# A Sinkhorn-sorted attention followed by a mixer: a fixed VectorE order, later channel results, one spin tile and split row sums

## The chip, the core and the metric

The kernel runs on one core of a Trainium2 chip. A core has TensorE (PE: matmuls, with weight loads listed apart as PEld), VectorE (DVE), ScalarE (ACT), GpSimd (POOL) and SyncE (SP), which run side by side, each with its own queue, and 16 DMA engines. The metric is device time in microseconds, as a median over runs. Before the change it is 265.28 us, the median of 6 runs (264.29 to 265.69).

## The reference

Four batches, eight heads, 768 positions, head width 64, model width 512. Cut to what matters:

```python
P = sort_net                                  # 4 x 8 x 8 x 8
for _ in range(5):
    P = np.exp(P - P.max(-1)); P = P / P.sum(-1); P = P / P.sum(-2)
k_sorted = einsum('bhij,bhjcd->bhicd', P, k_b)    # blocks of 96 positions, mixed by P
v_sorted = einsum('bhij,bhjcd->bhicd', P, v_b)
attn = softmax(q_b @ k_sorted.T / 8)              # within a block
x = attn @ v_sorted                               # then heads side by side: 4 x 768 x 512
a1 = alpha1 * x + beta1
u = x + lam * einsum('ts,bsd->btd', w_tok, a1)
a2 = alpha2 * u + beta2
out = u + lam * (relu(a2 @ w_ch1) @ w_ch2)        # hidden width 2048
```

## The kernel before

All of it is unrolled Python; there are no loops on the chip. The order of the work on an engine is either the order in which it is written (an `Engine` wrapper, L55 to L71, keeps it while its `fixed` is true) or, with `fixed` false and for DMAs on SP, chosen by a planner that simulates the program with its own costs. TensorE and POOL are in written order throughout. ScalarE is until L811. VectorE is until L817, `dve.fixed = False`; all that VectorE does after that, the planner orders. The planner also hands out the buffers.

PSUM has two pools: psA, two slots of two banks (`psa`), and psB, four slots of one bank (`psb`). Each tile takes a slot and keeps it until its last reader is done; the next tile that gets this slot waits for that.

**The head** (to about 42 us): five Sinkhorn rounds on a 32 x 8 x 8 tile (L244 to L265), with `spin` matmuls on TensorE whose result nobody reads, each group in a fresh psA tile. `mixing_heads` (L312) builds bigH, the mixing matrices of batch 0, in three pieces of 2, 2 and 4 heads, one at each `next`. For each of four pairs of heads (loop at L769), `mix_k0`/`mix_v0` mix keys and values on TensorE, and the results are copied out by ScalarE (first part) and VectorE (second); `sc0` computes scores and their exponential, `turn_v0` transposes values, and `pv0` multiplies by values and normalizes on VectorE (a reciprocal and a product) into `x_of[0]`. Then `prep_wtok` transposes w_tok by 128-column blocks, which `sort_wtok` has regrouped on POOL; `mixes(1, n)` mixes the values of batch 1 in three parts; `prep_rs` sums the rows of w_tok by 36 matmuls with a column of ones.

**The token half** of a batch (`moe_a`, or L790 to L816 for batch 0): six row tiles, each with `tok_part` (6 matmuls into psB), `moe_scale` and `moe_rest` (two VectorE operations; the second adds into the fp32 tile `u`, and ScalarE casts it to fp16). POOL has prepared `u` by `moe_rows` and `moe_start`. After three rows `moe_turn` transposes the fp16 tile, on TensorE for batch 0 and by DMA on SP for the others, and applies alpha2 and beta2: four VectorE operations that make a2T.

**The channel half**: `moe_h(b, hf)` computes 16 hidden tiles (4 matmuls each, relu on ScalarE); `moe_ch` has 16 matmuls per row tile, whose result VectorE multiplies by lam and adds to u, and SP stores.

**The weave** (L539): the channel half of batch b - 1 is a generator of units, and `weave` puts so many units (0.65 for a hidden tile, 0.216 for a channel matmul, in microseconds by the writer's count) between the steps of batch b's attention: key mixes, `scores(h4)`, `values(h4)`. `values` is, for each of two halves: matmuls, a reciprocal, products into x or xs; and for the last two groups three copies from xs to the last partitions of x (two on VectorE, one on ScalarE). Then `moe_a(b)` follows, and the rest of `moe_ch(b - 1, 1)`.

All operations are recorded by the wrapper, so that the profile gives one line, L65, for nearly all; tiles tell them apart: m_ps, k_ps, v_ps (mixes), sc_ps (scores), x_ps (values), tok_ps, h_ps, ch_ps, rs_ps, wtok_ps.

Of the kernel before, what the change touches and what calls it, by code (L numbers as in the profile page):

```python
# [1 line left out]

# [14 lines left out]
def kernel(  # L17
# [67 lines left out]
    def psa(shape, dtype, name):  # L85
        return psA.tile(shape, dtype, name=name, tag="psA")

    def psb(shape, dtype, name):
        return psB.tile(shape, dtype, name=name, tag="psB")
# [124 lines left out]
                    ident16[0:BH, 0:BH].rearrange("p (b h) -> p b h", h=H).unsqueeze(3).to_broadcast([BH, B, H, NB]),  # L214
                )

    def spin(ps, n):
        src = ident16[:].unsqueeze(1).to_broadcast([128, 4, 128])
        for _ in range(n):
            pe.matmul(ps, ident16[:], src, start=True, stop=True)  # L220


    def turn_q(b, h4, copy):
# [20 lines left out]
    for it in range(5):  # L244
        act.activation(P32[:], P32[:], AF.Exp)
        dve.tensor_reduce(rsum[:], P32[:], AXX, ALU.add)
        dve.reciprocal(rsum[:], rsum[:])
        dve.tensor_tensor(
            P32[:], P32[:], rsum[:].unsqueeze(2).to_broadcast([BH, NB, NB]), ALU.mult
        )  # L250
        dve.tensor_reduce(csum[:], P32[:].rearrange("p i j -> p j i"), AXX, ALU.add)
        dve.reciprocal(csum[:], csum[:])
        dve.tensor_tensor(
            (P16 if it == 4 else P32)[:], P32[:],
            csum[:].unsqueeze(1).to_broadcast([BH, NB, NB]), ALU.mult,
        )
        if it < 4:
            with nc.allow_low_precision(reason="sums of zeros and a one"):
                mask(it)
        if it == 2:  # L260
            prep_ab2()
        if it > 2:
            for h4 in ((0,), (1, 2, 3))[it - 3]:
                turn_q(0, h4, act.copy)
        spin(psa([128, 512], FT, "spin_ps")[:], (8, 0, 7, 4, 2)[it])  # L265

    def load_w1(gs):
        for g in gs:
# [43 lines left out]
    def mixing_heads():  # L312
        pjs = psb([NB, H, NB], FT, "pj_ps")
        for i in range(NB):
            pe.matmul(pjs[:, :, i], P16[:, i, :], ident16[0:BH, 0:H], start=True, stop=True)
        spin(psa([128, 512], FT, "spin_ps")[:], 1)
        pj = const([NB, H, NB], F16, "pj")
        dve.tensor_copy(pj[:], pjs[:])
        rep = psb([128, H, NB], FT, "rep_ps")
        pe.matmul(  # L320
            rep[:].rearrange("p h i -> p (h i)"), eb16[:].rearrange("p j r -> p (j r)"),
            pj[:].rearrange("p h i -> p (h i)"), start=True, stop=True,
        )
        spin(psa([128, 512], FT, "spin_ps")[:], 2)
        for hs in (slice(0, 2), slice(2, 4), slice(4, 8)):
            yield
            dve.tensor_tensor(
                bigH[:, hs, :, :],
                rep[:, hs, :].unsqueeze(3).to_broadcast([128, hs.stop - hs.start, NB, 16]),
                mskt[:].unsqueeze(1).unsqueeze(1).to_broadcast([128, hs.stop - hs.start, NB, 16]),  # L330
                ALU.mult,
            )
        yield
# [177 lines left out]
    def attention_steps(b, first, less=0.0):  # L511
# [24 lines left out]
        yield 2.4 - less, lambda: values(2)  # L536
        yield 2.4 - less, lambda: values(3)

    def weave(fill, steps):  # L539

        for gap, step in steps:
            filled = 0
            while filled < gap:
                took = next(fill, None)
                if took is None:
                    break
                filled += took
            step()

    w_tokT = const([128, NT, S], F16, "w_tokT")  # L550
# [21 lines left out]
            act.copy(dst[:, :, 0:96], pst[:, 0:TAIL].rearrange("p (kt x) -> p kt x", x=96))  # L572
            dve.tensor_copy(dst[:, :, 96:128], pst[:, TAIL:S].rearrange("p (kt x) -> p kt x", x=32))

    def prep_rs():
        rps = psb([128, NT], FT, "rs_ps")
        for kt in range(NT):
            for ks in range(NT):
                pe.matmul(
                    rps[:, kt:kt + 1], w_tokT[:, ks, kt * 128:(kt + 1) * 128], ones16[:],  # L580
                    start=(ks == 0), stop=(ks == NT - 1),
                )
        act.copy(rs[:], rps[:])

    u_of = {}
    u16_of = {}
# [58 lines left out]
    def moe_turn(b, hf, ps=psb):  # L645
        u16, a2T = u16_of[b], a2T_of[b]
        if b > 0:
            uT = uT_of[b][hf]
            for m in range(3):
                turned.append(nc.sync.dma_start_transpose(uT[:, :, m * 128:(m + 1) * 128], u16[:, 3 * hf + m, :]))  # L650
            for ci in range(CT):
                dve.tensor_scalar(
                    a2T[hf][:, ci, :], uT[:, ci, :], ab2col[:, ci:ci + 1], ab2col[:, CT + ci:CT + ci + 1],
                    op0=ALU.mult, op1=ALU.add,
                )
            return
        for cp in range(CT // 2):
            ups = ps([128, 2, 384], F16, "uT_ps")
            for cc in range(2):
                ci = 2 * cp + cc  # L660
                for m in range(3):
                    pe.transpose(
                        ups[:, cc, m * 128:(m + 1) * 128],
                        u16[:, 3 * hf + m, ci * 128:(ci + 1) * 128], ident16[:],
                    )
            for cc in range(2):
                ci = 2 * cp + cc
                if cp == 0:
                    act.activation(
                        a2T[hf][:, ci, :], ups[:, cc, :], AF.Identity,  # L670
                        bias=ab2col[:, CT + ci:CT + ci + 1], scale=ab2col[:, ci:ci + 1],
                    )
                else:
                    dve.tensor_scalar(
                        a2T[hf][:, ci, :], ups[:, cc, :], ab2col[:, ci:ci + 1], ab2col[:, CT + ci:CT + ci + 1],
                        op0=ALU.mult, op1=ALU.add,
                    )

    def moe_a(b):
        ahead = b + 1 if b < B - 1 else None  # L680
        moe_start(b)
        for kt in range(NT):
            if ahead and kt < 3:
                mixes(ahead, kt)
            tok_part(b, kt)
            moe_scale(b, kt)
            if kt % 3:
                moe_rest(b, kt - 1)
            if kt % 3 == 2:
                moe_rest(b, kt)  # L690
                moe_turn(b, kt // 3)
        if ahead:
            with tc.issue_after(turned[-1].ins):
                regroup_v(ahead)
# [3 lines left out]
    def moe_h(b, hf, which=range(HT)):  # L698
# [3 lines left out]
        for m in which:  # L702
# [4 lines left out]
                    start=(ci == 0), stop=(ci == CT - 1),  # L707
                )
            act.activation(hT_of[(b, hf)][m], hps[:], AF.Relu)
            yield 0.65  # L710

    def moe_ch(b, hf, kks=range(3)):
        hT = hT_of[(b, hf)]
        for kk in kks:
            kt = 3 * hf + kk
            last = b == B - 1 and kt == NT - 1
            u32 = u_of[(b, kt)]
            for lo, hi in ((0, 384), (384, C)) if last else ((0, C),):
                cps = psb([128, hi - lo], FT, "ch_ps")
                for m in range(HT):  # L720
# [2 lines left out]
                        start=(m == 0), stop=(m == HT - 1),  # L723
                    )
                    if m < HT - 1:
                        yield 0.216
                dve.tensor_tensor(cps[:], cps[:], lamB[:, lo:hi], ALU.mult)
                dve.tensor_tensor(u32[:, lo:hi], cps[:], u32[:, lo:hi], ALU.add)
                nc.sync.dma_start(out[b, kt * 96:(kt + 1) * 96, lo:hi], u32[0:96, lo:hi])
                (nc.scalar if last else nc.sync).dma_start(  # L730
                    out[b, TAIL + kt * 32:TAIL + (kt + 1) * 32, lo:hi], u32[96:128, lo:hi]
                )
                yield 0.216

    def run(units):
        for _ in units:
            pass


    ets = {}  # L740
# [10 lines left out]

    x_of[0] = moep.tile([128, NT, C], F16, name="x128", tag="x128", bufs=2)
    big = mixing_heads()
    for _ in range(3):
        next(big)
    k_copy, v_copy = mix_k0(0), mix_v0(0)
    k_copy(0, act.copy)
    k_copy(1, dve.tensor_copy)
    v_copy(0, act.copy)
    v_copy(1, dve.tensor_copy)  # L760
    next(big)
    load_raw(1, 1)
    load_w1(range(2))
    for n in range(3):
# [4 lines left out]
    for h4 in range(H4):  # L769
        sc0(h4)  # L770
        turn_v0(h4, dve.tensor_copy if h4 < 3 else act.copy)
        if h4 == 3:
            mixing_matrices(1, psb)
        if h4 > 0:
            pv0(h4 - 1, 0)
            pv0(h4 - 1, 1)
        if h4 < 3:
            k_copy, v_copy = mix_k0(h4 + 1), mix_v0(h4 + 1)
            k_copy(0, act.copy)
            k_copy(1, dve.tensor_copy)  # L780
            v_copy(0, act.copy)
            v_copy(1, dve.tensor_copy)
    prep_wtok(range(0, 2))
    pv0(3, 0)
    prep_wtok(range(2, 4))
    pv0(3, 1)
    prep_wtok(range(4, 6))
    mixes(1, 0)
    prep_rs()
    moe_rows(0, range(NT))  # L790
    moe_start(0)
    load_q(1)
# [21 lines left out]
        moe_scale(0, kt)  # L814
    for kt in (4, 5):
        moe_rest(0, kt)  # L816
    dve.fixed = False  # L817

    stack = ExitStack()
    for eng in order:  # L820
# [1 line left out]
    pe.fixed = True  # L822
    run(moe_h(0, 0, range(7)))
    moe_turn(0, 1)
    for n in range(3):
        mix_k(1, gs=(n,))
        run(moe_h(0, 0, range(7 + 3 * n, 9 + 3 * n)))
        turn_q(1, n, dve.tensor_copy)
        run(moe_h(0, 0, range(9 + 3 * n, 10 + 3 * n)))
    turn_q(1, 3, dve.tensor_copy)  # L830
    stack.close()
    pool.tensor_copy(gate[32:64, :], Vs[1][32:64, 0, 0:2])
# [11 lines left out]
    for b in range(1, B):  # L844
# [11 lines left out]
        moe_rows(b, range(5, NT))  # L856
        moe_a(b)
        run(moe_ch(b - 1, 1, (1, 2)))
        if b < B - 1:
            moe_rows(b + 1, range(3))  # L860
        if b == 1:
# [40 lines left out]
```

## Time and profile before

| | us |
|---|---|
| median of 6 runs | 265.28 |
| profiled execution, its own time | 264.45 |
| its span | 262.7 |
| TensorE busy | 249.9 |
| VectorE busy | 146.6 |
| ScalarE busy | 132.4 |
| POOL busy | 93.3 |
| TensorE busy of the first 42 us | 36.4 |

The span is the time from the first to the last instruction of one execution. A busy TensorE isn't TensorE at its peak, since matmuls overlap. A line of the timeline gives start, duration, engine, the operation with what it writes and reads, and in brackets the idle time of the engine before it and what ended that. A line of waits gives who waited for whom, and then the total, the number of times and the longest. The chain is the work that ended last, followed backwards. A wait for several things is put down to the one that came last, which is not always the one that was needed.

### The profile page before, as it was taken

What the parts mean: (1) busy time and instruction counts of PE and PEld (TensorE: products, weight loads), DVE (VectorE), ACT (ScalarE), POOL (GpSimd) and SP (SyncE); (2) the same over time, 40 slices, a digit from 0 to 9 for tenths busy, and PEclk for the clock granted to TensorE, in tenths of its full rate; (3) what the DMA queues carried; (4) which work ended last, traced back from release to release, by engine and by line L of the source; (5) the groups of instructions that cost most, each with busy time, mean ns of one, the idle gap of its engine ahead of it and who ended that gap; (6) DMA issues with size and microseconds to landing.
All of it is one profiled execution on the core that took longest, in us unless ns stands there. A gap on an engine that the chain in (4) does not pass through costs nothing.

```text
span 262.7 us, 5105 instructions
## 1 busy us (share of the span) xinstructions
PE 249.9 (95%) x2032; PEld 140.3 (53%) x2047; DVE 146.6 (56%) x323; ACT 132.4 (50%) x240; POOL 93.3 (36%) x101
## 2 busy tenths in 40 slices
PE   5988899999999799999999999999999999999993
PEld 1577645665555344554566445654665445545542
DVE  5776787682066796852625797644537973042033
ACT  3577887758622451484176632862574326505600
POOL 8433996000886395006830880203002700000000
PEclk9999999999999999999999999999999999999999
DMA  5999999999699734795999156991200342012012
GB/s 77 187 208 256 196 191 240 207 216 136 114 179 151 198 61 64 191 113 85 204 201 129 45 82 131 157 72 40 84 0 2 82 93 65 2 40 80 2 40 80
DMA packets 62327, 30.88 MB, mean 118 GB/s; under 512 B 48792, under 2 KB 58016, under 8 KB 62304
## 3 DMA queue, kind: packets, MB, share of 16 engines
q0 software_dynamic: 22912, 15.60, 40.4%
q1 hardware_dynamic: 39296, 14.90, 34.0%
q8 instruction: 16, 0.26, 0.4%
q10 hardware_dynamic: 96, 0.07, 0.1%
q14 instruction: 7, 0.06, 0.1%
HBM read 32.78 MB, written 8.65 MB: 158 GB/s over the span
## 4 chain that ended last, share of the span: by engine, by line
PE 74%; DMA 12%; DVE 8%; issue 2%; POOL 2%; ACT 1%; DVEq 0%; POOLq 0%
PE h_ps L65 31%; PE ch_ps L65 28%; DMA raw<-in_v_dram 10%; PE tok_ps L65 7%; DVE u L65 3%; PE sc_ps L65 2%; PE x_ps L65 2%; DVE tok_ps L65 2%; PE k_ps L65 1%; DMA a2T<-u 1%; DVE a2T L65 1%; PE v_ps L65 1%; PE q_ps L65 1%; DVE ch_ps L65 1%; POOL qn L65 1%
## 5 line engine op out<-in xcount | busy, mean ns | idle before, releaser
L65 PE MATMUL h_ps<-a2T,W1p 128*128 128x384 bf16 x512 | 89.0, 326 | 0.7 <-DVE u L65 0.6
L65 ACT ACTIVATE hT<-h_ps 128x384 bf16<-128x384 f32 x128 | 60.3, 492 | 55.6 <-PE h_ps L65 55.1
L65 PE MATMUL ch_ps<-W2p,hT 128*128 128x512 bf16 (+2 forms) x385 | 85.6, 370 | 1.0 <-issue 0.3
L65 PEld LDWEIGHTS <-W1p 128*128 128x128 bf16 x512 | 48.5, 98 | 32.5 <-issue 1.2
L65 PEld LDWEIGHTS <-hT 128*128 128x128 bf16 x400 | 37.6, 98 | 41.0
L65 DVE TENSOR_TENSOR ch_ps<-ch_ps,lamB 128x512 f32<-128x512 f32 (+2 forms) x25 | 16.9, 676 | 51.0 <-PE ch_ps L65 40.7
L65 POOL TENSOR_SCALAR u<-b1lB,rs 128x512 f32<-128x512 f32 x18 | 28.0, 1561 | 29.8 <-DMA out_dram<-u 23.4
L65 POOL TENSOR_TENSOR u<-x,u 128x512 f32<-128x512 f16 x22 | 25.3, 1182 | 29.2 <-DVE x L65 29.0
L65 PE MATMUL tok_ps<-x,w_tokT 128*128 128x512 f16 x144 | 32.9, 379 | 1.1 <-DVE x L65 1.1
L65 ACT ACTIVATE et<-sc_ps 96x768 f16<-96x768 f32 x32 | 24.0, 802 | 13.7 <-PE sc_ps L65 13.7
L65 ACT CAST u<-u 128x512 f16<-128x512 f32 x24 | 14.7, 618 | 20.9 <-DVE u L65 20.9
L65 PEld LDWEIGHTS <-w_tokT 128*128 128x128 f16 x180 | 15.0, 97 | 18.1 <-issue 1.4
L65 DVE CAST kT<-k_ps 64x512 f16<-64x512 f32 x30 | 20.6, 686 | 5.1 <-PE k_ps L65 4.7
L65 DVE RECIPROCAL recip<-x_ps 96x8 f32<-96x8 f32 (+1 forms) x32 | 6.2, 194 | 30.1 <-PE x_ps L65 30.1
L65 DVE TENSOR_TENSOR x<-x_ps,recip 96x512 f16<-96x512 f32 (+2 forms) x32 | 17.7, 554 | 1.0
L65 DVE TENSOR_TENSOR tok_ps<-tok_ps,a1lB 128x512 f32<-128x512 f32 x24 | 16.6, 693 | 2.6 <-PE tok_ps L65 2.6
L65 DVE TENSOR_TENSOR u<-tok_ps,u 128x512 f32<-128x512 f32 x24 | 16.4, 689 | 2.3 <-POOL u L65 0.7
L65 DVE TENSOR_TENSOR u<-ch_ps,u 128x512 f32<-128x512 f32 (+2 forms) x25 | 16.7, 670 | 0.8
L65 POOL DMA_DIRECT2D qn<-in_q_dram x16 | 14.0, 913 | 2.5 <-DMA raw<-in_v_dram 1.7
L65 POOL COPY gate<-Vs 32x2 f16<-32x2 f16 x2 | 0.4, 176 | 40.6 <-DMA Vs<-vscr 40.6
L65 PEld LDWEIGHTS <-et 96*128 96x128 f16 (+1 forms) x288 | 12.0, 105 | 3.0 <-DVE x L65 0.3
L65 PE MATMUL x_ps<-Vs,et 96*128 96x65 f16 (+1 forms) x288 | 12.7, 197 | 0.3 <-DVE xs L65 0.2
(88 smaller groups left out, 181.9 us busy)
## 6 DMA issues: line engine op xcount, KB each, us to landing
out_dram<-u SPq DMA_DIRECT2D x23, 192.0 KB, 2.4
raw<-in_k_dram POOLq DMA_DIRECT2D x8, 384.0 KB, 9.6
raw<-in_v_dram POOLq DMA_DIRECT2D x8, 384.0 KB, 8.0
vscr<-vA SPq DMA_DIRECT2D x6, 384.0 KB, 5.1
Vs<-vscr SPq DMA_DIRECT2D x6, 384.0 KB, 8.9
W1p<-in_moe_w_ch_dram POOLq DMA_DIRECT2D x4, 512.0 KB, 13.7
W2p<-in_moe_w_ch_dram POOLq DMA_DIRECT2D x4, 512.0 KB, 16.8
qn<-in_q_dram POOLq DMA_DIRECT2D x4, 384.0 KB, 8.6
```

What stands on the lines that cost most here:

```text
L65: ins = getattr(self.eng, name)(*args, **kwargs)
```

## The change

`dve.fixed = False` is gone, so that VectorE runs in written order to the end. What is taken of a channel tile is now a job of its own, `finish`; in the weave a job is written only once 1.2 (in the units' count) has gone by after the tile's last matmul. `moe_affine` is split from `moe_turn` for batches 1 to 3: half 0 is written behind all six rows, half 1 behind the last two channel tiles of the batch before. All spin matmuls write one tile, `rep` moves from psB to psA, and the k copies of the first pair of heads stand ahead of bigH's last two pieces. In the head's loop the next pair's key mix stands between the two halves of `pv0`, and the first block of w_tok is transposed there in the last turn. The row sums run over blocks in the outer loop, four blocks before `mixes(1, 0)` and two after it; only the first of the 36 matmuls has the start flag. Between 42 and 60 us one hidden tile comes ahead of the first key mix of batch 1, and none is left between the last two `turn_q`.

```diff
-    def spin(ps, n):
+    idle = psa([128, 512], FT, "spin_ps")
+    def spin(n):
...
-            pe.matmul(ps, ident16[:], src, start=True, stop=True)
+            pe.matmul(idle[:], ident16[:], src, start=True, stop=True)
...
-        rep = psb([128, H, NB], FT, "rep_ps")
+        rep = psa([128, H, NB], FT, "rep_ps")
...
+    late = []
+
+    def settle(took=None):
+        for job in late:
+            job[0] = 0 if took is None else job[0] - took
+        while late and late[0][0] <= 0:
+            late.pop(0)[1]()
+
+    def advance(unit, lag):
+        took, job = unit
+        settle(took)
+        if job:
+            late.append([lag, job])
+        return took
+
     def weave(fill, steps):
...
-                took = next(fill, None)
-                if took is None:
+                unit = next(fill, None)
+                if unit is None:
                     break
-                filled += took
+                filled += advance(unit, 1.2)
             step()
...
-    def prep_rs():
-        rps = psb([128, NT], FT, "rs_ps")
-        for kt in range(NT):
-            for ks in range(NT):
+    def prep_rs(rps, part):
+        for ks in part:
+            for kt in range(NT):
                 pe.matmul(
                     rps[:, kt:kt + 1], w_tokT[:, ks, kt * 128:(kt + 1) * 128], ones16[:],
-                    start=(ks == 0), stop=(ks == NT - 1),
+                    start=(ks + kt == 0), stop=(ks + kt == 2 * NT - 2),
                 )
-        act.copy(rs[:], rps[:])
+        if part[-1] == NT - 1:
+            act.copy(rs[:], rps[:])
...
 in moe_turn, for b > 0:
-            for ci in range(CT):
-                dve.tensor_scalar(
-                    a2T[hf][:, ci, :], uT[:, ci, :], ab2col[:, ci:ci + 1], ab2col[:, CT + ci:CT + ci + 1],
-                    op0=ALU.mult, op1=ALU.add,
-                )
             return
...
+    def moe_affine(b, hf):
+        uT, a2T = uT_of[b][hf], a2T_of[b][hf]
+        for ci in range(CT):
+            dve.tensor_scalar(
+                a2T[:, ci, :], uT[:, ci, :], ab2col[:, ci:ci + 1], ab2col[:, CT + ci:CT + ci + 1],
+                op0=ALU.mult, op1=ALU.add,
+            )
...
 in moe_a, behind the six rows:
+        moe_affine(b, 0)
...
+    def finish(b, kt, cps, lo, hi):
+        u32 = u_of[(b, kt)]
+        last = b == B - 1 and kt == NT - 1
+        dve.tensor_tensor(cps[:], cps[:], lamB[:, lo:hi], ALU.mult)
+        dve.tensor_tensor(u32[:, lo:hi], cps[:], u32[:, lo:hi], ALU.add)
+        nc.sync.dma_start(out[b, kt * 96:(kt + 1) * 96, lo:hi], u32[0:96, lo:hi])
+        (nc.scalar if last else nc.sync).dma_start(
+            out[b, TAIL + kt * 32:TAIL + (kt + 1) * 32, lo:hi], u32[96:128, lo:hi]
+        )
...
 in moe_ch, whose six lines from the product to the stores are gone:
-                        yield 0.216
+                        yield 0.216, None
+                yield 0.216, partial(finish, b, kt, cps, lo, hi)
...
     def run(units):
-        for _ in units:
-            pass
+        for unit in units:
+            advance(unit, 0.0)
+        settle()
...
     big = mixing_heads()
-    for _ in range(3):
-        next(big)
+    next(big)
+    next(big)
     k_copy, v_copy = mix_k0(0), mix_v0(0)
     k_copy(0, act.copy)
     k_copy(1, dve.tensor_copy)
+    next(big)
+    next(big)
     v_copy(0, act.copy)
     v_copy(1, dve.tensor_copy)
-    next(big)
...
     for h4 in range(H4):
         sc0(h4)
         turn_v0(h4, dve.tensor_copy if h4 < 3 else act.copy)
-        if h4 == 3:
-            mixing_matrices(1, psb)
         if h4 > 0:
             pv0(h4 - 1, 0)
+        if h4 < 3:
+            k_copy = mix_k0(h4 + 1)
+            k_copy(0, act.copy)
+            k_copy(1, dve.tensor_copy)
+        else:
+            mixing_matrices(1, psb)
+            prep_wtok(range(0, 1))
+        if h4 > 0:
             pv0(h4 - 1, 1)
         if h4 < 3:
-            k_copy, v_copy = mix_k0(h4 + 1), mix_v0(h4 + 1)
-            k_copy(0, act.copy)
-            k_copy(1, dve.tensor_copy)
+            v_copy = mix_v0(h4 + 1)
             v_copy(0, act.copy)
             v_copy(1, dve.tensor_copy)
-    prep_wtok(range(0, 2))
+    prep_wtok(range(1, 2))
     pv0(3, 0)
     prep_wtok(range(2, 4))
     pv0(3, 1)
     prep_wtok(range(4, 6))
+    rps = psb([128, NT], FT, "rs_ps")
+    prep_rs(rps, range(4))
     mixes(1, 0)
-    prep_rs()
+    prep_rs(rps, range(4, NT))
...
-    dve.fixed = False
...
     run(moe_h(0, 0, range(7)))
     moe_turn(0, 1)
+    run(moe_h(0, 0, range(7, 8)))
     for n in range(3):
         mix_k(1, gs=(n,))
-        run(moe_h(0, 0, range(7 + 3 * n, 9 + 3 * n)))
+        run(moe_h(0, 0, range(8 + 3 * n, 10 + 3 * n)))
         turn_q(1, n, dve.tensor_copy)
-        run(moe_h(0, 0, range(9 + 3 * n, 10 + 3 * n)))
+        run(moe_h(0, 0, range(10 + 3 * n, min(11 + 3 * n, HT))))
     turn_q(1, 3, dve.tensor_copy)
...
         moe_a(b)
         run(moe_ch(b - 1, 1, (1, 2)))
+        moe_affine(b, 1)
```

## The prediction

> **What bounds the kernel now.** I first read the page: busy time by engine, then the slices.
>
> ```profile
> PE 249.9 (95%) x2032; PEld 140.3 (53%) x2047; DVE 146.6 (56%) x323; ACT 132.4 (50%) x240; POOL 93.3 (36%) x101
> PEclk9999999999999999999999999999999999999999
> ```
>
> TensorE is busy for 249.9 of 262.7 us, and its granted clock stays at the top, so nothing is to be had from the clock. No edit takes matmuls away, so what can be won is idle TensorE time: 12.8 us. The busy time by stretch says where it lies:
>
> ```profile
> 20.00:31.00 11.00, 9.48 (x193) 7.96 (x190) 8.19 (x26) 8.71 (x15) 7.08 (x8) 1.00 1.11 235
> ...
> 60.00:85.00 25.00, 24.63 (x221) 13.79 (x223) 8.76 (x22) 12.06 (x23) 15.35 (x16) 1.00 1.33 141
> 85.00:108.50 23.50, 21.52 (x120) 10.43 (x121) 18.56 (x38) 9.73 (x15) 12.97 (x10) 1.00 0.55 121
> 108.50:146.00 37.50, 37.32 (x318) 21.60 (x321) 19.08 (x40) 20.73 (x40) 12.85 (x15) 1.00 1.19 145
> ```
>
> The first pair of numbers is the stretch and its length, the next TensorE's busy time. From 108.5 us to 258 it is idle for 0.55 us (0.18, 0.05, 0.16, 0.05 and 0.11 by stretch), and 4.0 us at the end are the last results on their way out. Only one stretch after the head has a hole, 85 to 108.5 us: 1.98 us. The head, up to 42 us, holds the other 5.7. Then the waits of TensorE, by what ended them:
>
> ```profile
> PE tok_ps L65 <- DVE x L65: 1.1, 1, 1.1
> PE h_ps L65 <- DVE u L65: 0.6, 1, 0.6
> PE v_ps L65 <- DMA raw<-in_v_dram: 0.6, 1, 0.6
> ```
>
> Three single waits, each in its own place: the first token matmul of batch 1 (at 89.18 us), one hidden tile of batch 2's weave (at 108.52) and batch 1's first value mix (at 31.38). The chain shows the last:
>
> ```profile
> 13.99 17.35 DMA raw<-in_v_dram
> 31.33 0.04 issue
> 31.38 0.61 PE v_ps L65 x2
> 31.98 0.91 PE rs_ps L65 x36
> 32.89 1.32 PE tok_ps L65 x6
> ```
>
> The load of batch 1's values lands at 31.33, whatever TensorE does before; the head is bound by that load, not by the engines.
>
> **Part 1: row sums split.** Before, TensorE ends its last w_tok transpose at 30.79 (29.90 plus 0.89 in the timeline), waits 0.59 for the load, mixes, and only then does 36 row-sum matmuls, 0.91 us by the chain or 25 ns each. After, 24 of them come ahead of the mix: 24 x 25 = 0.61 us, from 30.79 to 31.40. So the wait is filled, and tok_part(0, 0) starts at 31.38 + 0.44 + 12 x 25 ns = 32.1 instead of 32.75: **0.6 us**. This needs the first four blocks of w_tokT; their last copy ends at 30.79 on VectorE. Is the 0.6 kept? The u rows hang on the ScalarE copy of rs, queued behind the copy of the mix, and that copy doesn't move (32.02 to 33.03); so VectorE's first scaling stays at 34.55. But its second waits for TensorE (0.73 us before 35.97), and can start at 35.4; from there rows, casts and the turn at 40.09 all move by 0.57. POOL's rows (35.25, 36.5, ...) are early enough.
>
> Here the Trainium skill speaks against the move. "TensorE: Matmul & The Clock Gate", section "LDWEIGHTS (loading the stationary operand)", gives columns / 1.2 ns for a weight load, 107 ns for 128 columns, and every row-sum matmul has a load of its own. By that, 24 take 2.56 us, the mix would slip by 2.0 us to 33.4, the rs copy with it, and the gain would turn into a loss of about 1.4. The rows of weight loads read 97 ns each in fact, but they overlap: 36 went through in 0.91 us. I take the measured 25 ns.
>
> **Part 2: the head's reordering** (rep in the psA pool, k copies ahead of bigH's later heads, pv0's halves interleaved, first w_tok block earlier). In the loop, score to score takes 3.63 us (17.17, 20.80, 24.44), for 3.0 us of TensorE work; the score waits for the VectorE copy of kT, which is queued behind two attention results (0.70 each: 0.22 plus 0.47 start to start). With one of them moved behind that copy, I estimate 0.5 us less in each of two turns. Against it: the first score's second half now needs the slot that rep holds until bigH's last part. That part is 0.68 us and moves ahead of the v copy (k copy at 13.91, then 0.34, 0.35 and 0.68 to 15.3), so the first score ends at 15.6 instead of 15.2, and the transposes behind it at 16.2 instead of 15.9: 0.3 lost. Bounds on TensorE's arrival at the mix: 0.3 later to 1.1 earlier (w_tok's last regrouping on POOL ends at 28.70, and 12 transposes after it take 0.89). **Zero** in the sum, since an early arrival only waits for the load; a late one would eat as much of part 1's 0.6. The single spin tile costs nothing: its matmuls are a warm-up on one engine, and one slot is as good as two in turn.
>
> **Part 3: one hidden tile ahead of batch 1's key mix** (42 to 60 us). The same 64 matmul groups of 0.65 us, otherwise ordered. It moves the first q transposes by 0.65 - 0.57, from 49.66 to 49.74; the weight load there ended a wait on the qn load, so without this the earlier clock of part 1 would be lost there. At the end two q turns stand back to back: two 0.59 us pieces of TensorE beside two 0.56 us copies. Zero.
>
> **Part 4: VectorE in written order, channel results six matmuls later** (6 x 0.216 = 1.296, over the lag of 1.2). I counted where each result now stands among the attention steps. In batches 2 and 3 every one stands where the profile already has it: the first two before the values of group 0, the third before group 1, the fourth after group 3. In batch 1 two move. Before, VectorE takes the third channel product at 82.83 ahead of the reciprocal, and the fourth at 88.19 ahead of the copies that the token matmul waits for:
>
> ```profile
> 82.83 0.70 DVE L65 TENSOR_TENSOR ch_ps<-ch_ps,lamB 128x512 f32<-128x512 f32 x1 [2.21 <-PE ch_ps L65]
> ...
> 87.86 0.41 DVE L65 TENSOR_TENSOR xs<-x_ps,recip 96x256 f16<-96x256 f32 x1
> 88.19 0.68 DVE L65 TENSOR_TENSOR ch_ps<-ch_ps,lamB 128x512 f32<-128x512 f32 x1
> 88.90 0.47 DVE L65 COPY x<-xs 32x256 f16<-32x256 f16 x2
> ```
>
> After, the fourth stands behind the copies (0.70 less), but the third stands between group 2 and group 3, still ahead of them. The row starts at 83.02 (x_ps at 82.56 plus the 0.46 of the other groups). By start-to-start distances: group 2 0.23 + 0.61 + 0.22 + 0.35 + 0.37, copies 0.75, third result 0.73 + 0.61, group 3 0.23 + 0.61 + 0.22 + 0.35 + 0.44, first copy 0.28: 6.00, so the token matmul starts at 89.02 instead of 89.18. **0.16 us**, not the 1.15 that the wait is worth: VectorE is the bound in these six microseconds. TensorE's 0.15 us wait at 85.81 falls within it.
>
> **Part 5: moe_affine moved.** Before, the second affine stands ahead of the second channel result:
>
> ```profile
> 105.89 1.25 DVE L65 TENSOR_SCALAR a2T<-a2T,ab2col 128x384 bf16<-128x384 f16 x4 [3.00 <-DMA a2T<-u]
> 107.05 0.70 DVE L65 TENSOR_TENSOR ch_ps<-ch_ps,lamB 128x512 f32<-128x512 f32 x1
> 107.78 0.69 DVE L65 TENSOR_TENSOR u<-ch_ps,u 128x512 f32<-128x512 f32 x1
> ```
>
> VectorE waits 3.00 us for a transposing DMA while the channel matmuls ended at 104.7; the slot is freed at 108.47, and TensorE starts its next hidden tile at 108.52. After, the result is taken at 104.75 to 106.15, and the tile need not wait: **0.6 us**. In batches 2 and 3 nothing waited here: 0. What stands behind the affine's wait now: the affine itself and the key copies (at 108.39 before). With the first affine behind the sixth row, the last cast starts at 99.8 instead of 101.48, so the transposes land nearer 104.1 than 105.8. The first affine ends at 101.1 instead of 100.85, against a first use at 104.7 - 0.7.
>
> **Sum:** 0.6 + 0.16 + 0.6 = 1.36 us, 262.7 to 261.3 of span. The profiled execution took 264.45, 1.75 around its span; the same step from there is 263.1. The six runs' median of 265.28 lies 0.83 above that execution, so I put the step on the median: **263.9 us**.
>
> **Rivals.** (a) *The full wait goes.* If the third result, too, falls outside the row before the token matmul, 1.15 goes instead of 0.16: 262.9. For it: it is the largest of the three waits. Against: the count above puts that result six matmuls after its last, four ahead of group 3. (b) *Part 1 is lost again*, at the qn load (49.66, no slack beyond 0.1) or through a late head: 0.76 stays, 264.5. (c) *It doesn't do what it says*: the POOL row at 89.30, which waits for an output store that the transposes on SP hold back until 86.52, stays where it is; its u row is first used at 92.03. If the slots behind it bind, all gains up to there end there. Against: the fifth token tile, at 94.5, needs its slot at 92.7, so 1.8 us are to spare. That gives 265.3. (d) *Slower: the SP queue and the strict order meet.* SP's order is still a plan. If it sets the store of the second channel result ahead of the second three transposes, they can issue only from 105.5, take 3 x 1.86 (11.18 for six) and 1.2 to land: 112.3. The affine (1.25) and three key copies (2.08) behind it then end at 115.6, and the third key mix, at 113.59 - 1.36 = 112.2, needs their slot: 3.4 lost, 2.0 net, 267.3. It decides once the landing passes 108.9, 3.1 us later than now. Against: casts are ready before that result.
>
> **How the numbers follow.** A measurement tells this kernel from no change at about 0.3%, 0.8 us: faster is below 264.48, slower above 266.08. Chances: the forecast 0.54, its own range 263.3 to 264.5; (a) 0.10; (b) 0.14, half of it under the bound; (c) 0.11; (d) 0.11. So faster 0.54 + 0.10 + 0.07 = 0.71, same 0.07 + 0.11 = 0.18, slower 0.11. Leaving out (d) and the lower half of (a), the range is 262.8 to 265.5: above (c) by 0.2 for the spread of the runs.
>
> **What would show it.** Right: tok_ps starting near 32.1; no wait of v_ps longer than before with 24 row sums ahead of it; tok_ps of batch 1 still waiting for VectorE, about 1 us, near 88.4; no h_ps wait on u near 107; batches 2 and 3 the same length. Wrong: a v_ps mix later than 31.5; a q_ps wait on qn; key copies waiting behind a2T for a transpose; longer stretches after 110 us.

## The result

The changed kernel takes 263.41 us, the median of its runs (262.24 to 267.66), against 264.65 for the kernel before beside it: a ratio of 0.9953, with a 95% interval of 0.9939 to 0.9967. Forecast were 263.9 against 265.28, a ratio of 0.9948. The profiled execution took 263.21, with a span of 261.4; the sum on record gave 263.1 and 261.3. The total is right; below it shows that several of its terms were not, and that they offset each other by luck. In five of the changed kernel's executions, the ones above 266 us, TensorE's mean granted clock was 0.985 to 0.990; a median "at full clock" below is one of executions with a mean of 0.995 or more.

The page after, busy time and granted clock:

```profile
PE 248.8 (95%) x2032; PEld 140.4 (54%) x2047; DVE 146.0 (56%) x323; ACT 133.1 (51%) x240; POOL 93.2 (36%) x101
PEclk9999999999999999999999999999999999999999
```

The work is the same, 2032 matmuls. Busy time by stretch, with the same columns as before (the stretch, its length, then TensorE first):

```profile
20.00:31.00 11.00, 9.47 (x203) 8.43 (x204) 8.38 (x27) 8.41 (x13) 6.11 (x8) 1.00 1.12 236
...
60.00:85.00 25.00, 24.63 (x223) 13.99 (x226) 9.25 (x26) 12.55 (x23) 15.35 (x16) 1.00 1.34 144
85.00:108.50 23.50, 22.25 (x127) 10.89 (x128) 19.92 (x38) 9.78 (x16) 12.92 (x10) 1.00 0.63 140
108.50:146.00 37.50, 37.34 (x318) 21.45 (x320) 18.86 (x41) 21.31 (x41) 14.09 (x16) 1.00 1.16 136
```

Between 85 and 108.5 us TensorE is idle for 1.25 us instead of 1.98. The weave of batch 2 behind it is as full as it was. The waits of TensorE, by what ended them:

```profile
PE v_ps L66 <- DMA raw<-in_v_dram: 0.7, 1, 0.7
PE v_ps L66 <- DVE x L66: 0.6, 1, 0.6
PE tok_ps L66 <- DVE x L66: 0.5, 1, 0.5
```

The wait of h_ps for VectorE is gone. The load wait is still there, longer by 0.1, and the wait of 1.15 before the first token matmul now stands in two pieces, 0.60 and 0.54. Where TensorE stands at the same point of the work, read from its timelines:

| point | before | after | gap | won or lost since the row above |
|---|---|---|---|---|
| first token matmul, batch 0 | 32.75 | 32.92 | +0.17 | 0.17 lost |
| first hidden tile | 42.05 | 42.23 | +0.18 | 0 |
| first score of batch 1 | 60.33 | 60.01 | -0.32 | 0.50 won |
| first token matmul, batch 1 | 89.18 | 88.64 | -0.54 | 0.22 won |
| second half's hidden tiles | 104.71 | 104.30 | -0.41 | 0.13 lost |
| third key mix of batch 2 | 113.59 | 112.35 | -1.24 | 0.83 won |
| span | 262.7 | 261.4 | -1.3 | 0.06 won |

The sum on record had 0.6 won in the first row, nothing in the third, 0.16 in the fourth and 0.6 in the sixth.

### The profile page after: what moved, and what is told of

Its sections match the earlier page's. It is cut to its first block, busy times and chain, and to the rows that moved or that the text cites. A ratio compares the mean times of both kernels' runs of the same rounds, so it can differ in the third digit from the quotient of the medians.

```text
span 261.4 us, 5106 instructions
## 1 busy us (share of the span) xinstructions
PE 248.8 (95%) x2032; PEld 140.4 (54%) x2047; DVE 146.0 (56%) x323; ACT 133.1 (51%) x240; POOL 93.2 (36%) x101
## 4 chain that ended last, share of the span: by engine, by line
PE 76%; DMA 11%; POOL 7%; DVE 3%; issue 2%; POOLq 0%; DVEq 0%
PE ch_ps L66 30%; PE h_ps L66 30%; PE tok_ps L66 9%; DMA wt<-in_moe_w_tok_dram 7%; DMA qn<-in_q_dram 4%; PE sc_ps L66 2%; PE x_ps L66 2%; POOL wtp L66 2%; POOL raw L66 2%; POOL u L66 2%; PE k_ps L66 1%; DVE x L66 1%; PE q_ps L66 1%; PE v_ps L66 1%; POOL qn L66 1%
## 5 line engine op out<-in xcount | busy, mean ns | idle before, releaser
L66 ACT ACTIVATE et<-sc_ps 96x768 f16<-96x768 f32 x32 | 24.0, 802 | 12.8 <-PE sc_ps L66 12.8
L66 DVE TENSOR_TENSOR u<-tok_ps,u 128x512 f32<-128x512 f32 x24 | 15.8, 684 | 1.4 <-POOL u L66 1.1
L66 ACT CAST vA<-v_ps 128x1024 f16<-128x1024 f32 x9 | 9.0, 1008 | 8.3 <-PE v_ps L66 8.3
```

The lines of the kernel that those rows point to most:

```text
L66: ins = getattr(self.eng, name)(*args, **kwargs)
```

## The experiments

The theory is the sum on record: the split, the third result and the affine bring the gain, and parts 2 and 3 nothing. The rivals: the split is worth nothing where TensorE is late anyway, part 2 costs something, and part 3 brings something.

**No split** (no_split). All 36 row sums behind the mix:

```diff
+    mixes(1, 0)
     rps = psb([128, NT], FT, "rs_ps")
-    prep_rs(rps, range(4))
-    mixes(1, 0)
-    prep_rs(rps, range(4, NT))
+    prep_rs(rps, range(NT))
```

> The changed kernel with all 36 row sums behind the value mix again. Theory (part 1: 24 row sums of 25 ns fill a wait for the value load): token part of batch 0 starts 24 x 25 ns = 0.6 us later after the mix, the time is 0.6 us more than the changed kernel's, so about 0.6 less than before (ratio 0.9975 to before). Rival (the load's own scatter or the head's order hides it): same time as the changed kernel, ratio about 0.995.

263.72 us, ratio 0.998 (0.9943 to 1.0016); at full clock 263.20 (eight of twelve), no worse than the changed kernel's 263.35. The profile says why nothing was lost. TensorE's timeline in the changed kernel first, then in this one:

```profile
30.08 0.83 PE L66 MATMUL wtok_ps<-ident,wtp 128*128 128x128 f16 x12
30.75 0.74 PE L66 MATMUL rs_ps<-ones,w_tokT 128*128 128x1 f16 x24
32.18 0.61 PE L66 MATMUL v_ps<-raw,bigV 128*128 128x512 f16 x2 [0.69 <-DMA raw<-in_v_dram]
32.62 0.44 PE L66 MATMUL rs_ps<-ones,w_tokT 128*128 128x1 f16 x12
32.92 1.46 PE L66 MATMUL tok_ps<-x,w_tokT 128*128 128x512 f16 x6
```

```profile
29.27 0.49 PE L66 MATMUL wtok_ps<-ident,wtp 128*128 128x128 f16 x6 [0.96 <-DVE w_tokT L66]
...
31.58 0.59 PE L66 MATMUL v_ps<-raw,bigV 128*128 128x512 f16 x2
32.01 1.26 PE L66 MATMUL rs_ps<-ones,w_tokT 128*128 128x1 f16 x36
33.14 1.02 PE L66 MATMUL tok_ps<-x,w_tokT 128*128 128x512 f16 x4
```

In the changed kernel the row sums do run inside the wait, of which 0.69 us is left, and token work starts 0.74 after the mix instead of the 1.37 before the change. But here there is no wait to fill: TensorE itself is late, because it waited 0.96 us for VectorE at 29.27. VectorE's timeline in the same kernel, and POOL's:

```profile
27.27 1.27 DVE L66 TENSOR_TENSOR bigP<-mskb,red 128x128 f16<-128x128 f16 x1
28.46 0.58 DVE L66 TENSOR_TENSOR bigV<-mskv,red 128x128 f16<-128x128 f16 x1
28.97 0.24 DVE L66 COPY w_tokT<-wtok_ps 128x192 f16<-128x192 f16 x1
```

```profile
24.18 4.72 POOL L66 COPY wtp<-wt 128x1152 f16<-128x1152 f16 x6 [4.04 <-DMA wt<-in_moe_w_tok_dram]
...
27.25 1.14 POOL L66 COPY wtp<-wt 128x1152 f16<-128x1152 f16 x1
```

bigP, a product of two SBUF tiles, takes 1.27 us. Its two later instances in the changed kernel take 0.29. Of POOL's six copies in the first row one runs beside it, from 27.25 to 28.39 (second row), and bigP ends 0.14 later. In the changed kernel's own profile the copies begin 0.7 us later, and bigP and bigV take 0.41 and 0.59. bigP took 1.16 to 1.27 in no_split, affine_between and third_result_later, and 0.49 in old_hidden_order (the last three stand further down). The new theory: VectorE and POOL exclude each other here, and what that costs depends on when w_tok lands.

**A shorter POOL copy** (short_pool_copies), which should let VectorE in sooner if it waits only for the running instruction: each of the six copies is written as three (the larger ones of 128 x 1152 as 128 x 384, the smaller ones of 128 x 384 as 128 x 128).

```diff
-            pool.tensor_copy(
-                t_[:, :, :, lo:hi],
...
+            for ts in (slice(0, 2), slice(2, 4), slice(4, 6)):
+                pool.tensor_copy(
+                    t_[:, ts, :, lo:hi],
```

> The changed kernel with each of POOL's six w_tok copies cut in three. Theory (a VectorE product with both inputs in SBUF waits until the running POOL copy ends): no bigP over 0.75 us, the w_tok transpose's wait falls by about half a microsecond, if the cut copies don't take longer in all; ratio 0.992 to 0.995. Rival (bigP waits for something else): bigP still takes about 1.2 us in some executions, ratio 0.995 or more.

The opposite. Six of its eleven executions took 263.1 to 264.0 us (a ratio of 0.995, 0.9931 to 0.9968, no gain on the changed kernel's 0.9953), and five took 269.0 to 269.8 with a clock of 0.973 to 0.979. The profile is of one of these five; of the six there is none. VectorE's and POOL's timelines:

```profile
27.29 4.56 DVE L66 TENSOR_TENSOR bigP<-mskb,red 128x128 f16<-128x128 f16 x1
31.77 0.28 DVE L66 TENSOR_TENSOR bigV<-mskv,red 128x128 f16<-128x128 f16 x1
```

```profile
27.13 2.12 POOL L66 COPY wtp<-wt 128x384 f16<-128x384 f16 x6
29.21 1.27 POOL L66 TENSOR_TENSOR a1lB<-a1lB,lamB 128x512 f32<-128x512 f32 x1
30.44 1.26 POOL L66 TENSOR_TENSOR b1lB<-b1lB,lamB 128x512 f32<-128x512 f32 x1
```

One VectorE instruction was kept out for 4.56 us, past eight POOL instructions that stood back to back, until the last ended near 31.7. TensorE waited 3.95 us for the copies behind it. The Trainium skill, "SBUF — State Buffer", section "Who interferes with whom", states the lock: a VectorE instruction with two inputs in SBUF and a GpSimd one that reads SBUF exclude each other, for the whole instruction. The no_split rows agree (1.27 us beside a copy of 1.14). The page's summary has the second block "until the first finishes"; here that was a copy that ended at 27.64, 0.36 us after bigP's start. Nine other profiles agree with it: wherever bigP stood beside POOL's copies, it ended 0.14 us after the POOL instruction that was running when it came up, though the next one followed at once. The 4.56 show that it can also last as long as POOL has a next instruction ready. Why it got in at the first gap there and not here is open.

**One SBUF input less** (sums_in_psum). If the lock is the cause, bigP and bigV of batch 1 must be quick once their second input comes from PSUM:

```diff
-        red = att.tile([128, NB], FT, name="red", tag="red", bufs=2)
+        red = rep[:, 0:NB] if b == 1 else att.tile([128, NB], FT, name="red", tag="red", bufs=2)
```

> The changed kernel with the sums from which batch 1's bigP and bigV are made written to PSUM instead of SBUF, so that these products have one input in SBUF and not two. All else, POOL's copies and the order too, is the changed kernel's. Theory (a product with two inputs in SBUF is kept out while POOL reads SBUF): bigP and bigV take 0.3 to 0.4 us each beside POOL's copies, no w_tok transpose waits over 0.3 us, the runs don't scatter above 264; ratio 0.990 to 0.9925. Rival (any VectorE instruction that writes or reads SBUF is kept out, or the output is what blocks): bigP still takes up to 1.2 us, ratio 0.995.

262.76 us, 0.9911 (0.9878 to 0.9944). VectorE's timeline:

```profile
27.55 0.29 DVE L66 TENSOR_TENSOR bigP<-mskb,rep_ps 128x128 f16<-128x128 f16 x1
27.76 0.28 DVE L66 TENSOR_TENSOR bigV<-mskv,rep_ps 128x128 f16<-128x128 f16 x1
```

At the same place, among the same POOL copies (one runs from 27.02 to 28.17), both run at full speed: that two SBUF inputs are what meets POOL is shown. The profiled execution, one of the longer of the six, had another hole: 0.97 us in the middle of a value product at 28.42, for which it shows no cause, so its span (261.6) doesn't show the gain of the median.

**The matrices early** (early_matrices). `mixing_matrices(1, psb)` at the first turn of the loop, 16.4 us, before POOL's copies begin:

```diff
         sc0(h4)
+        if h4 == 0:
+            mixing_matrices(1, psb)
         turn_v0(h4, dve.tensor_copy if h4 < 3 else act.copy)
...
         else:
-            mixing_matrices(1, psb)
             prep_wtok(range(0, 1))
```

> The changed kernel with batch 1's mixing matrices made in the first turn of the head's loop, before w_tok lands and POOL starts its copies. Theory (bigP, 0.29 us alone, took 1.16 to 1.27 us in three profiles of the changed head, up to the end of the POOL copy that was running, and a w_tok transpose waited 0.84 to 0.96 us behind it): bigP and bigV take 0.3 us each, that wait falls under 0.3, the first token matmul of batch 0 starts at 32.1 to 32.4 instead of 33.1; ratio to before 0.991 to 0.9935. Rival (the wait has another cause, a slot or ScalarE): the wait stays, ratio about 0.995.

262.15 us, 0.990 (0.9878 to 0.9921), and the least spread of all: 262.05 to 262.74. bigP takes 0.29. TensorE's timeline:

```profile
30.52 0.74 PE L66 MATMUL rs_ps<-ones,w_tokT 128*128 128x1 f16 x24
31.12 0.59 PE L66 MATMUL v_ps<-raw,bigV 128*128 128x512 f16 x2
31.55 0.66 PE L66 MATMUL rs_ps<-ones,w_tokT 128*128 128x1 f16 x12
32.08 1.46 PE L66 MATMUL tok_ps<-x,w_tokT 128*128 128x512 f16 x6
```

Token work starts where part 1 had forecast it, 32.08 against 32.1, but by two differences that cancel: the mix came at 31.12 instead of 31.38, and the last 12 row sums took 0.53 instead of 0.30.

**The same without the split** (early_no_split). The two edits shown, together.

> The kernel with early matrices, and all row sums behind the value mix again. Theory (part 1 of the prediction, in a head that arrives before the load lands): the row sums filled a wait, so the first token matmul of batch 0 starts 0.3 to 0.6 us later and the ratio is 0.991 to 0.9925. Rival (the head arrives after the load has landed anyway): same as with the split, 0.990, no wait of v_ps.

263.17 us, 0.9937 (0.991 to 0.9963). The wait for the load is back, 1.06 us before the mix at 31.82, and token work starts at 33.16. Between this and the one above lies 1.0 us of median, 0.9 at full clock (263.09), with ratios whose intervals overlap. But 0.70 of the 1.08 between the two profiles is the load, which landed at 31.82 here and by 31.12 there; from the mix to the token work it is 1.34 against 0.96. So the split is worth something where the head is on time for it, 0.4 in these two profiles; that it is worth its 0.6 is not shown.

**The old head** (old_head). Part 2 undone: rep in psB, the k copies behind bigH's third piece, pv0's halves together, the matrices ahead of pv0.

```diff
-    next(big)
-    next(big)
+    for _ in range(3):
+        next(big)
...
-        if h4 < 3:
-            k_copy = mix_k0(h4 + 1)
-            k_copy(0, act.copy)
-            k_copy(1, dve.tensor_copy)
-        else:
-            mixing_matrices(1, psb)
-            prep_wtok(range(0, 1))
```

> The changed kernel with the old head: rep in psB, bigH's first two parts ahead of the key copies, both halves of pv0 together, mixing matrices ahead of pv0, w_tok blocks 0 and 1 after the loop; the split of the row sums stays. My prediction gave part 2 nothing as long as the value load is the bound: same as the changed kernel, 0.995, first token matmul of batch 0 at 32.1. Rival (part 2 costs what the profiles show, 0.8 us of arrival, since it puts bigP into POOL's copies): this kernel is 0.4 to 0.9 us faster than the changed one, ratio 0.9915 to 0.9935.

262.68 us, 0.9913 (0.9887 to 0.994): 0.4% better than with part 2, with intervals that just touch. The profile does not show where: bigP took 0.92 us in it, and the token work started at 33.17 (its whole head ran late in that execution: first score at 15.23, against 14.56 in vector_order_alone with the same head).

**Part 3 undone, and part 3 alone** (old_hidden_order, hidden_order_alone). The one hidden tile behind the first key mix again, in the changed kernel; and ahead of it, in the kernel before.

```diff
-    run(moe_h(0, 0, range(7, 8)))
...
-        run(moe_h(0, 0, range(8 + 3 * n, 10 + 3 * n)))
+        run(moe_h(0, 0, range(7 + 3 * n, 9 + 3 * n)))
...
-        run(moe_h(0, 0, range(10 + 3 * n, min(11 + 3 * n, HT))))
+        run(moe_h(0, 0, range(9 + 3 * n, 10 + 3 * n)))
```

> The changed kernel with the hidden tiles of batch 0 in their old order around the key mixes and query turns. My prediction gave part 3 nothing: same as the changed kernel, ratio about 0.995, and perhaps 0.1 for the query load. New theory from the two profiles (the stretch from the first hidden matmul to the first score of batch 1 takes 17.78 us instead of 18.28, since two query turns back to back take 0.93 us instead of twice 0.59, with one hand-over less of 0.11, and the key mix no longer stands directly behind the transposes, 0.27): 0.5 us more than the changed kernel, ratio about 0.997.

265.59 us, 1.0003 (0.997 to 1.0036); at full clock 263.60 (six of twelve), 0.25 above the changed kernel's. From the first hidden tile to the first score of batch 1 it took 41.66 to 59.93, or 18.27, against 17.78 in the changed kernel and 18.28 before.

> The kernel before with batch 0's hidden tiles reordered (part 3) and nothing else. Theory (one hand-over less between query turns and hidden tiles, and no key mix directly behind the transposes): the stretch from the first hidden matmul to the first score of batch 1 is 0.5 us shorter; ratio 0.998. Prediction on record: nothing, ratio 1.000.

264.33 us, 0.9979 (0.9956 to 1.0003), and 44.62 to 62.26, or 17.64, in the profile. TensorE's timeline at the last query turns, before the change and then in this kernel:

```profile
55.86 0.66 PE L65 MATMUL q_ps<-ident,qn 128*64 128x128 f16 x12
56.46 0.82 PE L65 MATMUL h_ps<-a2T,W1p 128*128 128x384 bf16 x4
```

```profile
57.41 1.46 PE L65 MATMUL h_ps<-a2T,W1p 128*128 128x384 bf16 x8
58.80 1.00 PE L65 MATMUL q_ps<-ident,qn 128*64 128x128 f16 x24
59.73 0.82 PE L65 MATMUL h_ps<-a2T,W1p 128*128 128x384 bf16 x4
```

Two query turns back to back take 0.93 from start to start. Before, each took 0.60 (55.86 to 56.46, 57.21 to 57.81): 0.27 more. A hidden tile of four matmuls before a turn takes 0.75 instead of the 0.65 that it takes among its like: 0.10 for one change of work more. These 0.37 are all that the order is shown to give: with the old order vector_order_alone took 41.95 to 59.96, or 18.01. The other 0.27 of the 0.64 lie at the first key mix behind the transposes of u. It came 0.94 after their start before and in old_hidden_order, but 0.67 in vector_order_alone, as the hidden tile that stands there now does; what held it in those two profiles they do not show. Of the new order, seven of the eleven kernels show 17.64 or 17.65.

**The VectorE order alone** (vector_order_alone): parts 4 and 5 and the spin tile, with head, row sums and hidden order as before.

> The kernel before with the VectorE edits alone (written order, later channel results, affine moved; and the shared spin tile): the row sums, the head and batch 0's hidden tiles are as before. Theory: 0.16 (token row) and 0.6 to 0.76 (hidden tile) remain, 0.8 to 0.9 us, ratio 0.9965; waits of TensorE as in the kernel before up to 80 us. Rival (they need the earlier clock of the other parts, or cost elsewhere): ratio 0.998 to 1.001.

263.06 us, 0.9947 (0.9923 to 0.9971): as much as the whole change. The three edits of TensorE's order add nothing to it in sum.

**The affine earlier** (affine_between). The second affine ahead of the last channel tile:

```diff
-        run(moe_ch(b - 1, 1, (1, 2)))
+        run(moe_ch(b - 1, 1, (1,)))
         moe_affine(b, 1)
+        run(moe_ch(b - 1, 1, (2,)))
```

> The changed kernel with the second affine written between the two channel tiles, as VectorE had it before. Theory (part 5: the channel result behind the affine holds the slot of a hidden tile): a wait of a hidden tile for VectorE's u comes back near 107 us, about 0.6 us and up to 0.16 more for refilling; ratio about 0.9975 to 0.998. Rival (the slot is handed out otherwise in this program, or the transposes land early enough): no wait, ratio about 0.995.

263.7 us, 0.9973 (0.9952 to 0.9993). TensorE's timeline before the change, in this kernel, then in the changed one:

```profile
105.81 2.11 PE L65 MATMUL h_ps<-a2T,W1p 128*128 128x384 bf16 x12
108.52 1.46 PE L65 MATMUL h_ps<-a2T,W1p 128*128 128x384 bf16 x8 [0.60 <-DVE u L65]
```

```profile
108.37 1.46 PE L66 MATMUL h_ps<-a2T,W1p 128*128 128x384 bf16 x8 [0.62 <-DVE u L66]
...
113.44 0.61 PE L66 MATMUL k_ps<-bigP,raw 128*128 128x128 f16 x8
```

```profile
105.40 3.41 PE L66 MATMUL h_ps<-a2T,W1p 128*128 128x384 bf16 x20
108.65 0.61 PE L66 MATMUL k_ps<-bigP,raw 128*128 128x128 f16 x8
109.10 3.41 PE L66 MATMUL h_ps<-a2T,W1p 128*128 128x384 bf16 x20
112.35 0.61 PE L66 MATMUL k_ps<-bigP,raw 128*128 128x128 f16 x8
```

The wait is back where it was (0.62 before 108.37, against 0.60 before 108.52). VectorE again stood 2.16 us before the affine for the transposing DMA, with the channel result behind it. That this order is what made TensorE wait is shown.

**The third result later** (third_result_later). The lag in batch 1's weave doubled, which is rival (a) made true:

```diff
-        weave(fill, steps)
+        weave(fill, steps, 2.4 if b == 1 else 1.2)
```

(`weave` hands the number on to `advance`.)

> The changed kernel with the lag at 2.4 instead of 1.2 in batch 1's weave alone, so that VectorE takes the third channel result behind the values of the last group. Theory (VectorE is the bound in the six microseconds ahead of batch 1's first token matmul): its row is 1.34 us shorter, so the two waits ahead of that matmul (0.60 and 0.54 us) nearly go, TensorE is 0.7 to 1.1 us earlier there; ratio 0.991 to 0.993. Rival (POOL's u rows, first used at 92.0 whatever TensorE does, hold the slots of the fifth token tile): the gain comes back as a wait of a later token tile, ratio about 0.994 to 0.995.

262.4 us, 0.9924 (0.9893 to 0.9954). VectorE's timeline, the changed kernel and then this one:

```profile
84.56 0.72 DVE L66 COPY x<-xs 32x768 f16<-32x768 f16 x2
85.20 0.68 DVE L66 TENSOR_TENSOR ch_ps<-ch_ps,lamB 128x512 f32<-128x512 f32 x1
85.92 0.69 DVE L66 TENSOR_TENSOR u<-ch_ps,u 128x512 f32<-128x512 f32 x1
86.53 0.19 DVE L66 RECIPROCAL recip<-x_ps 96x8 f32<-96x8 f32 x1
```

```profile
84.61 0.72 DVE L66 COPY x<-xs 32x768 f16<-32x768 f16 x2
85.43 0.20 DVE L66 RECIPROCAL recip<-x_ps 96x8 f32<-96x8 f32 x1
```

Token work starts at 87.56 instead of 88.64, 1.08 earlier, and the waits there fall from 1.14 to 0.19. Nothing behind it gives the time back.

**Both** (early_and_later). Early matrices and the doubled lag together.

> The changed kernel with both edits that gained: batch 1's mixing matrices in the first turn of the head, and in batch 1 a lag of 2.4. Theory (they lie in different stretches and both are on TensorE's path): the gains add up, 0.990 and 0.7 to 1.1 us, ratio 0.986 to 0.988, and the runs lie close together as with the early matrices alone. Rival (an earlier clock meets POOL's u rows or the query load): ratio 0.989 to 0.991, with a new wait of a later token tile.

262.11 us, 0.9886 (0.9845 to 0.9927): by ratio a little better than either edit alone (0.990 and 0.9924), within an interval that spans both, and no better by median than the early matrices (262.15). TensorE's timeline says where the second gain went:

```profile
86.63 1.46 PE L66 MATMUL tok_ps<-x,w_tokT 128*128 128x512 f16 x6 [0.18 <-DVE x L66]
...
93.54 2.75 PE L66 MATMUL tok_ps<-x,w_tokT 128*128 128x512 f16 x12 [0.70 <-DVE u L66]
```

The token work is 2.0 us ahead of the changed kernel's, and its fifth tile waits for the slot that POOL's u row holds, which waited 6.75 us for an output store until 90.07. That is rival (c)'s POOL row, which was said to bind once more than 1.8 us are won before it.

## Why the prediction was right

The sum of 1.36 us was met (1.3 of span, 1.24 of median), but partly by luck: part 1's 0.6 didn't arrive in the profile, and 0.5 came from part 3, which the sum put at nothing. Parts 4 and 5 were right in mechanism. (One reading was off by little: of the 12.8 us idle the head holds 5.6, and another 0.6 lies between 42 and 85 us, which the list leaves out.)

- **Part 1, 0.6.** The mechanism is right: the 24 row sums took 0.74 us by their row (0.60 from start to start in early_matrices), the mix did not wait for them, and 0.63 less lies between the mix and the token work. By the weight-load rule that spoke against it they would have taken 2.56; the measured 25 to 31 ns each stand. What failed is "the head is bound by that load": in the profile the load came 0.8 us later than before and took the gain with it. That is scatter: the load ended at 32.44 in hidden_order_alone, which has the head of before, and by 31.12 in early_matrices. And TensorE is late in some profiles, with either head, when the split has nothing to fill: its transposes ended at 31.58 in no_split and at 31.79 in old_head.
- **Part 2, zero.** Wrong by old_head's median: against it the changed kernel loses 0.4%, about 1 us, with intervals that just touch. The estimate of 0.5 in each of two turns came true once (score to score 3.07 in the first); in the second it was 3.54, with a new wait of 0.43 for the VectorE copy of vT. The step that failed is "**Zero** in the sum, since an early arrival only waits for the load": it costed the turns and not what VectorE meets at the end of the last one, where bigP had taken 0.48 at 26.25 before, beside 0.29 for its later instances. But this lock doesn't tell the two heads apart: bigP took 0.48, 0.91, 0.92 and 1.11 in the four profiles with the old head and 0.41, 0.49, 1.16, 1.24 and 1.27 in five with the new, and the w_tok transposes ended at 30.79 to 31.79 with the old and at 30.75 to 31.58 with the new. So early_matrices and sums_in_psum (0.990, 0.9911) show what it is worth to take the lock away, and not what part 2 cost: the old head meets the lock as well. What part 2 itself lost, and where, stays open.
- **Part 3, zero.** Wrong by 0.5 in the profiles (by medians hidden_order_alone gains 0.2%, in an interval that includes none): "The same 64 matmul groups of 0.65 us, otherwise ordered" left out what a change from one kind of work to another costs, 0.37 of it shown. Of the 0.64 between the profiles before and of hidden_order_alone, 0.15 went to the qn load: q_ps at 50.36 is 1.54 after the hidden tiles before it, instead of 1.39. The prediction had named that wait as a danger.
- **Part 4, 0.16.** Right: 0.22, with the third result between group 2 and group 3 as counted, and 1.14 of wait left against "about 1 us". VectorE is the bound there, as the doubled lag showed.
- **Part 5, 0.6.** Right in mechanism, and too small: 0.83. Idle time fell by 0.60, but a wait costs more than its idle time. Before, twelve hidden matmuls from 105.81 would have given way at 107.76 (12 x 0.1625, the step inside a group), and the next started at 108.52: 0.76. The row's 2.11 counts the last matmul to its end, and those 0.16 are lost as well; the last 0.07 lie between the second and third key mix. Against it stand 0.13 lost just ahead.
- **Rivals.** (a) is not what happened, but the speed was there. (b) came true in part: 0.15 went at the qn load, as it says, but part 1's gain was taken in the profile by the value load, which it doesn't name. (d) didn't come: the transposes had landed before VectorE came to the affine at 105.98. (c) showed only in early_and_later.

## What to carry to other kernels

Before moving a VectorE operation with two SBUF inputs, look at what POOL is doing at the new time: the same row at two durations in a trace (0.29 and 0.48 here) is the sign. An in-order engine should take results in the order in which someone waits for them, and one transposing DMA ahead of a ready result is enough to stall another engine. And a sum that comes out right needs its parts measured too: here VectorE's order alone gave as much as the whole change, and the rest was a loss and gains that offset each other.

## What was not expected of the hardware

A VectorE instruction of 0.29 us can be held for 4.56 us behind a run of POOL instructions (short_pool_copies), though in nine other profiles it got in behind the first.

TensorE's granted clock halves after a hole much shorter than was expected. In hidden_order_alone the load landed late, and TensorE's timeline and its busy time by stretch (the clock is the last but two) show:

```profile
32.44 0.60 PE L65 MATMUL v_ps<-raw,bigV 128*128 128x512 f16 x2 [1.42 <-DMA raw<-in_v_dram]
```

```profile
29.60:33.00 3.40, 1.98 (x36) 1.55 (x34) 1.88 (x7) 2.24 (x4) 3.40 (x5) 1.00 1.07 175
...
33.50:34.00 0.50, 0.50 (x18) 0.41 (x16) 0.00 (x0) 0.50 (x2) 0.46 (x1) 0.50 1.10 154
...
35.00:36.00 1.00, 1.00 (x4) 0.41 (x3) 0.69 (x2) 1.00 (x2) 0.95 (x1) 0.50 1.23 202
...
37.00:38.00 1.00, 1.00 (x6) 0.49 (x5) 0.26 (x1) 0.76 (x1) 1.00 (x2) 1.00 1.25 209
```

A hole of 1.42 us, with TensorE busy for 1.98 of the 3.40 us before 33.0, was followed by three microseconds at a clock of 0.50: six token matmuls took 2.52 from start to the next mix instead of 1.30. In the changed kernel the same 3.40 us have 2.71 busy, and the clock held. The busy share alone doesn't decide it: in no_split TensorE is busy for 1.93 of the 3.40 us from 26.60 to 30.00, and the clock held too. The Trainium skill, "TensorE: Matmul & The Clock Gate", section "HAM oscillation — how this bites in real kernels", asks for no gap above about 3.4 us; by that this one was harmless, and the measurement decides. In short_pool_copies, where the hole was 3.95 us, the clock stood at 0.50 from 30 to 40. Means below 0.990 were seen in the changed kernel, no_split, old_hidden_order, third_result_later and short_pool_copies, which all have bigP and bigV beside POOL's copies at 27.3 us (so has affine_between, where none of twelve was), and in one of 78 executions of the kernel before. That such a hole in the head is what lowers the clock in the changed kernel's is likely, but there is no trace of one of these.
